# An mLSTM with a feed-forward layer: from chunk 8 on the state's part of the rows stays in PSUM

## The chip, the cores and the metric

The kernel runs on 1 core of one Trainium2 chip. The metric is the device time in microseconds (us), taken as the median over runs of the whole kernel. Engines are called by their short names: PE (TensorE, matmul), PEld (its weight loads), DVE (VectorE), ACT (ScalarE), POOL (GpSimd), SP (SyncE, which here only issues DMAs).

## What is computed

The reference, cut to its recurrence: 4 batches, 8 heads, 768 tokens, head width 40.

```python
for t in range(S):
    m_new = np.maximum(f_gate[:, :, t] + m, i_gate[:, :, t])
    f_stab = np.exp(f_gate[:, :, t] + m - m_new)
    i_stab = np.exp(i_gate[:, :, t] - m_new)
    m = m_new
    C = f_stab * C + i_stab * einsum('bhd,bhe->bhde', vt, kt)
    n = f_stab * n + i_stab * kt
    h_tilde = einsum('bhde,bhe->bhd', C, qt)
    nq = einsum('bhd,bhd->bh', n, qt)
    denom = np.maximum(np.abs(nq), 1.0)
    y[:, :, t] = sigmoid(o_gate[:, :, t]) * h_tilde / denom
...
h = x @ w_in                       # x: y as 3072 tokens x 320
g = np.maximum(h, 0.0) + alpha * np.minimum(h, 0.0)
return g @ w_out                   # 320 -> 2048 -> 320
```

## The kernel before

**Chunks and groups.** The recurrence is done in 24 chunks of 128 tokens (6 to a batch; `n` is the chunk, `c` its place in the batch). Within a chunk the rows come from decay-weighted scores, and what went before the chunk comes from a carried state. Two chunks make a group `g` of 256 tokens, and the feed-forward layer runs over 12 groups, in 8 steps of 256 features each: `up` (L563) makes 16 matmuls into one bank `ph`, then ACT, two DVE instructions at L585, ACT (`gh`, L593) and POOL (`gl`, L594) split the result, and `down` (L597) adds 12 matmuls per step into the two banks `po`.

**One chunk of attention from chunk 8 on** (`stage_b`, L402). For each half of the heads (`par`) ACT makes the decays `E` (L419), POOL masks them (L423), PE makes the scores `pS` (L435), DVE weighs them (L325), and ACT and DVE split them into three bf16 parts (L327, L328). Then `from_state` (L350) lets PE multiply the queries with the carried state into the PSUM bank `pI` (L364), and DVE scales that by the decay `eT` into the SBUF tile `T` (L367; a column of `eT` for each head is repeated over the 42 columns of the head). `values_by_parts` (L331) makes the rows of the chunk itself in two banks `pH` (L340), and DVE reduces these into the SBUF tile `S` (L344). L452 adds `S` to `T`. `gated_steps` (L378) takes the two columns of each head that carry plus and minus the denominator, takes the maximum of both and 1 (`r`, L386 in one instruction; where `c` is 0 there is no state, the rows are `S` alone, and L388 and L389 do it in two), takes the reciprocal (L390), multiplies it into the output gate `og` (L393, on POOL from chunk 6 on), and multiplies the rows with the gate into `xn` (L395, on DVE from chunk 8 on). POOL copies the last 64 columns of `xn` (L399). After a group's second chunk `stage_x` (L489) transposes `xn` on PE into two banks `p1`, `p2` (L463), and ACT and DVE split these (L482 to L486) for the feed-forward layer.

**Buffers.** All PSUM banks of the attention come from `psa` (L33): it takes two tags in turn, and each tag has two banks. So the fourth `psa` tile after a `pI` has the tag of `pI` again, and so has the second. A chunk takes them in this order: `pS` for par 0, [`p1`, `p2` of the group before], `pS` for par 1, `pI`, `pH` 0, `pH` 1, then `pu` of the next chunk's state update (L156). The SBUF tag `T` has two buffers, which `T`, `S` and `vr` (L313, the rest of the values of the next chunk, made on POOL at L315) share.

**Order of the work.** Attention runs as a side stream of the feed-forward layer (`Side`, L1113, and the loops from L1129): it goes two groups or so ahead. The order in which each engine issues its instructions is fixed when the program is built: a scheduler takes the instructions by priority, with durations that it estimates, and hands out a tag's buffers as they come free. On the chip every engine then follows its list in that order.

Of the kernel before, what the change touches and what calls it, by code (L numbers as in the profile page):

```python
# [8 lines left out]
F32 = mybir.dt.float32  # L9
# [4 lines left out]
ALU = mybir.AluOpType  # L14
# [3 lines left out]
def kernel(ctx: ExitStack, tc: tile.TileContext, q, k, v, i_gate, f_gate, o_gate, w_in, w_out, alpha, out):  # L18
    nc = tc.nc
    B, H, S, D = q.shape  # L20
    DM, DFF = w_in.shape
    P = 128
# [7 lines left out]
    VA = D + 2  # L30
# [4 lines left out]
    sb = ctx.enter_context(tc.tile_pool(name="sb", bufs=2))  # L35
# [6 lines left out]
    def psa(name):  # L42
        turns.reverse()
        return ps_a.tile([P, 512], F32, tag=turns[0], name=name)
# [34 lines left out]
    eT = const.tile([P, NC, BH], F32, tag="eT", name="eT")  # L79
# [131 lines left out]
    def state_parts(n):  # L211

        return C_t[2 - n % 2].rearrange("p h e -> p (h e)").bitcast(BF16).rearrange("p (s x) -> p s x", s=2)
# [81 lines left out]
    def values(n, E, busy=lambda: None):  # L295

        pH = psa(f"pH{n}")
        va = va_t[n // GC % NV][:, n % GC]
        for i in range(H):
            if i % 2 == 0:  # L300
                busy()
            par, p = divmod(i, NPR)
            h = 2 * p + par
            nc.tensor.matmul(
                pH[:, h * VA : (h + 1) * VA], E[par][:, p * P : (p + 1) * P], va[:, h], start=True, stop=True
            )
        return pH[:, : H * VA].rearrange("p (h e) -> p h e", e=VA)

    def value_parts(n):

        va = va_t[n // GC % NV][:, n % GC]
        V = late_pool.tile([P, H, 3, VA], BF16, tag="t", name=f"vb{n}", bufs=3)
        rest = sb.tile([P, H, VA], F32, tag="T", name=f"vr{n}")  # L313
        nc.scalar.copy(V[:, :, 0], va)
# [16 lines left out]
    def values_by_parts(n, Es):  # L331


        V = vbs.pop(n)
        S = sb.tile([P, H, VA], F32, tag="T", name=f"S{n}")
        for par in range(2):
            pH = psa(f"pH{n}_{par}")
            for p in range(NPR):
                for k, e in enumerate(Es[par]):
                    nc.tensor.matmul(  # L340
                        pH[:, p * 3 * VA : (p * 3 + 3 - k) * VA], e[:, p * P : (p + 1) * P],
                        V[:, 2 * p + par, : 3 - k], start=k == 0, stop=k == 2,
                    )
            nc.vector.tensor_reduce(  # L344
                by_parity(S, par), pH[:, : NPR * 3 * VA].rearrange("p (r k e) -> p r e k", k=3, e=VA),
                mybir.AxisListType.X, ALU.add,
            )
        return S

    def from_state(n, qf, Q=None):  # L350

        b, c = divmod(n, NC)
        pI = psa(f"pI{n}")
        if b == 0:
            C = C_t[(n - 1) % 3][:R].rearrange("p h e -> p (h e)")
            for p in range(NPR):
                es = slice(2 * p * VA, 2 * (p + 1) * VA)
                nc.tensor.matmul(pI[:, es], qf[:R, p * P : (p + 1) * P], C[:, es], start=True, stop=True)
        else:
            C = state_parts(n - 1)[: 3 * D]  # L360
            for h in range(H):
                es = slice(h * VA, (h + 1) * VA)
                for s in range(2):
                    nc.tensor.matmul(pI[:, es], Q[: 3 * D, s, h], C[:, s, es], start=s == 0, stop=s == 1)  # L364
        yield
        T = sb.tile([P, H, VA], F32, tag="T", name=f"T{n}")
        nc.vector.tensor_tensor(  # L367
            T, pI[:, : H * VA].rearrange("p (h e) -> p h e", e=VA),
            eT[:, c, b * H : (b + 1) * H].unsqueeze(2).broadcast_to([P, H, VA]), ALU.mult,
        )  # L370
        yield T

    def gated(n, hv):

        for _ in gated_steps(n, hv):
            pass

    def gated_steps(n, hv):  # L378
        b, c = divmod(n, NC)
        g, j = divmod(n, GC)  # L380
        if j == 0:
            xn_tiles[g] = sb.tile([P, GC, DM + KR], F32, tag="xn", name=f"xn{g}")
        xn = xn_tiles[g]
        r = sb.tile([P, H], F32, tag="r", name=f"r{n}")
        if c > 0:
            nc.vector.scalar_tensor_tensor(r, hv[:, :, D], 1.0, hv[:, :, D + 1], ALU.max, ALU.max)  # L386
        else:
            nc.vector.tensor_scalar(r, hv[:, :, D], 1.0, None, ALU.max)  # L388
            nc.vector.tensor_tensor(r, r, hv[:, :, D + 1], ALU.max)  # L389
        nc.vector.reciprocal(r, r)  # L390
        yield
        sg = o_tiles[b][:, c]
        (nc.gpsimd if n in SGP else nc.vector).tensor_tensor(sg, sg, r.unsqueeze(2).broadcast_to([P, H, D]), ALU.mult)  # L393
        yield
        (nc.gpsimd if c > 0 and n in XNP else nc.vector).tensor_tensor(  # L395
            xn[:, j, :DM].rearrange("p (h d) -> p h d", d=D), hv[:, :, :D], sg, ALU.mult
        )
        yield
        nc.gpsimd.tensor_copy(xn[:, j, DM:], xn[:, j, 2 * P : DM])  # L399
        yield  # L400

    def stage_b(n):  # L402
# [45 lines left out]
        if c > 0:  # L448
            *_, T = from_state(n, qf, Q)
        hv = values(n, Es) if n < NBF else values_by_parts(n, Es)  # L450
        if c > 0:
            nc.vector.tensor_tensor(T, T, hv, ALU.add)  # L452
            hv = T
# [82 lines left out]
    NBF = 8  # L536
# [253 lines left out]
    def first_group():  # L790
# [189 lines left out]
        def state_part():  # L980
            it = from_state(1, qk[1][0])
            next(it)
            yield
            got["T"] = next(it)
            yield
# [67 lines left out]
        add("u0m u0c", update_steps(0))  # L1053
        add("fsm fst", state_part())
        add("g0r g0g g0x g0p", lazily(lambda: gated_steps(0, got["h0"])))
        add("g1r g1g g1x g1p", lazily(lambda: gated_steps(1, got["T"])))
        add("s0a s0d", lazily(lambda: split_steps(0, slice(0, P), p1[0], p2[0])))
        add("s1a s1d", lazily(lambda: split_steps(0, slice(P, GT), p1[0], p2[0])))
# [132 lines left out]
```

## Time and profile before

| what | value |
|---|---|
| runs of the kernel before | 517.74, 509.68, 512.25 us; median 512.25 |
| the profiled execution | 514.26 us; span from its first to its last instruction 512.5 us |
| mean granted TensorE clock in it | 0.973 of full speed |
| busy share of PE, PEld, DVE, ACT, POOL | 96%, 91%, 65%, 62%, 59% |

Of a profiled execution every instruction has a start and a duration. "Idle before, releaser" tells how long the engine stood idle before an instruction and what ended that. Line numbers (L367) are those of the kernel before.

### The profile page before, as it was taken

The numbers are of one execution on the slowest core, as the hardware profiler recorded it, in microseconds if no ns is written. First come the engines' busy times: TensorE is split into PE (matmuls) and PEld (weight loads), VectorE is DVE, ScalarE is ACT, GpSimd is POOL, SyncE is SP. The second block draws the span as 40 slices with busy tenths as digits, with TensorE's granted clock in tenths as the row PEclk, the third lists the DMA queues.
The fourth block names the chain that finished last, engine by engine and source line by source line (L and its number), as shares of the span: only waits on it lengthen the run. The fifth ranks groups of instructions, "written<-read, shape, count | busy, mean of one in ns | idle before, by whom it ended". The sixth has DMA issues, their size and how long they took to land.

```text
span 512.5 us, 11748 instructions
## 1 busy us (share of the span) xinstructions
PE 490.2 (96%) x4455; PEld 469.0 (91%) x4455; DVE 334.3 (65%) x648; ACT 317.3 (62%) x687; POOL 304.2 (59%) x385
## 2 busy tenths in 40 slices
PE   8889989999999989999899999999998999999997
PEld 7778979999999989999789999999887999999997
DVE  7868999855444696785585687776676686652321
ACT  3839698655385667776976677686774664433332
POOL 6631154032197788859579789768866956333242
PEclk9878997999999999999999999999997999999999
DMA  9967977275068466487484664767642050000000
GB/s 170 239 135 223 245 190 209 68 144 127 1 145 203 95 162 140 81 185 161 108 170 100 149 143 104 162 159 130 152 136 61 30 115 2 1 27 1 27 1 26
DMA packets 171518, 60.58 MB, mean 118 GB/s; under 512 B 137990, under 2 KB 163958, under 8 KB 171462
## 3 DMA queue, kind: packets, MB, share of 16 engines
q1 hardware_dynamic: 171382, 59.73, 52.2%
q8 instruction: 35, 0.57, 0.5%
q14 instruction: 21, 0.17, 0.1%
q10 hardware_dynamic: 80, 0.11, 0.1%
HBM read 36.90 MB, written 4.03 MB: 80 GB/s over the span
## 4 chain that ended last, share of the span: by engine, by line
PE 67%; DVE 9%; POOL 8%; DMA 6%; ACT 4%; issue 4%; SPq 1%; ACTq 0%; POOLq 0%; DVEq 0%
PE po L602 25%; PE ph L572 4%; PE ph L578 3%; PE ph L575 3%; PE ph L573 3%; PE ph L576 3%; PE ph L577 3%; PE ph L574 3%; PE ph L579 3%; DMA kS<-Z 2%; POOL gl L594 2%; PE pH L340 2%; PE warm L929 2%; DMA wo<-in_moe_w_out_dram 2%; PE pS L435 2%
## 5 line engine op out<-in xcount | busy, mean ns | idle before, releaser
L594 POOL TENSOR_TENSOR gl<-g,gh 128x512 fp32r<-128x512 f32 x80 | 103.8, 1297 | 60.9 <-ACT gh L593 51.4
L585 DVE SCALAR_TENSOR_TENSOR g<-g,oma,ph 128x256 f32<-128x256 f32 x160 | 69.5, 475 | 76.7 <-ACT g L581 76.3
L602 PE MATMUL po<-OH,gh 128*128 128x320 f32 x352 | 107.8, 318 | 0.5 <-ACT gh L593 0.5
L602 PE MATMUL po<-OL,gh 128*128 128x320 f32 x352 | 105.2, 311 | 0.0
L581 ACT ACTIVATE g<-ph 128x512 f32<-128x512 f32 x96 | 57.1, 595 | 54.8 <-PE ph L579 43.2
L593 ACT CAST gh<-g 128x512 fp32r<-128x512 f32 x80 | 49.5, 619 | 38.6 <-DVE g L585 38.3
L602 PE MATMUL po<-OH,gl 128*128 128x320 f32 x352 | 68.8, 316 | 0.7 <-POOL gl L594 0.7
L602 PEld LDWEIGHTS po<-OH,gh 128*128 128x128 f32 x352 | 66.6, 190 | 1.0 <-ACT gh L593 0.9
L602 PEld LDWEIGHTS po<-OL,gh 128*128 128x128 f32 x352 | 66.4, 189 | 0.2 <-DVE OL L701 0.2
L572 PE MATMUL ph<-XH,WH 128*128 128x256 f32 x192 | 59.2, 308 | 3.0 <-DVE r L390 2.1
L423 POOL TENSOR_SCALAR_AFFINE_SELECT E<-E 128x512 f32<-128x512 f32 x44 | 31.3, 713 | 42.3 <-ACT E L419 39.2
L602 PEld LDWEIGHTS po<-OH,gl 128*128 128x128 f32 x352 | 55.0, 190 | 1.2 <-POOL gl L594 1.1
L576 PE MATMUL ph<-X,W 128*128 128x256 f32 x192 | 55.1, 288 | 0.0
L578 PE MATMUL ph<-XL,WH 128*128 128x256 f32 x192 | 54.8, 286 | 0.0
L573 PE MATMUL ph<-XH,WH 128*128 128x256 f32 x192 | 54.8, 285 | 0.0
L419 ACT ACTIVATE E<-Lb,bT 128x128 f32<-128x128 f32 x160 | 51.0, 393 | 6.0 <-PE pH L340 5.4
L575 PE MATMUL ph<-XH,WL 128*128 128x256 f32 x192 | 54.7, 285 | 0.0
L577 PE MATMUL ph<-XL,WH 128*128 128x256 f32 x192 | 54.6, 285 | 0.0
L574 PE MATMUL ph<-XH,WL 128*128 128x256 f32 x192 | 54.6, 284 | 0.0
L579 PE MATMUL ph<-X2L,W 128*128 128x256 f32 x192 | 54.6, 285 | 0.0
L327 ACT CAST E<-pS 128x512 bf16<-128x512 f32 x64 | 36.9, 581 | 19.2 <-DVE pS L328 10.8
L572 PEld LDWEIGHTS ph<-XH,WH 128*128 128x128 f32 x192 | 36.7, 191 | 4.0 <-issue 2.3
(194 smaller groups left out, 1200.0 us busy)
## 6 DMA issues: line engine op xcount, KB each, us to landing
Lb<-L_d SPq DMA_DIRECT2D x20, 512.0 KB
wo<-in_moe_w_out_dram SPq DMA_DIRECT2D x8, 640.0 KB
wi<-in_moe_w_in_dram SPq DMA_DIRECT2D x8, 512.0 KB
qn<-in_q_dram SPq DMA_DIRECT2D x24, 160.0 KB
kn<-in_k_dram SPq DMA_DIRECT2D x24, 160.0 KB
va<-in_v_dram SPq DMA_DIRECT2D x24, 160.0 KB
og<-in_o_gate_dram SPq DMA_DIRECT2D x24, 160.0 KB
out_dram<-ob SPq DMA_DIRECT2D x11, 320.0 KB
```

What stands on the lines that cost most here:

```text
L572: nc.tensor.matmul(dst, WH[half][:, 0, hs], XH[:, 0], start=True, stop=False)
L573: nc.tensor.matmul(dst, WH[half][:, 1, hs], XH[:, 1], start=False, stop=False)
L574: nc.tensor.matmul(dst, WL[half][:, 0, hs], XH[:, 0], start=False, stop=False)
L575: nc.tensor.matmul(dst, WL[half][:, 1, hs], XH[:, 1], start=False, stop=False)
L576: nc.tensor.matmul(dst, W2[:, fs], X2, start=False, stop=False)
L577: nc.tensor.matmul(dst, WH[half][:, 0, hs], XL[:, 0], start=False, stop=False)
L578: nc.tensor.matmul(dst, WH[half][:, 1, hs], XL[:, 1], start=False, stop=False)
L579: nc.tensor.matmul(dst, W2[:, fs], X2L, start=False, stop=True)
L581: nc.scalar.activation(gt, ph, AF.Relu, scale=-1.0)
L585: nc.vector.scalar_tensor_tensor(out=y[:, e], in0=gt[:, e], scalar=oma[:, f : f + 1], in1=ph[:, e], op0=ALU.mult, op1=ALU.add)
L594: (nc.vector if g < 2 else nc.gpsimd).tensor_tensor(gl, y, gh.bitcast(F32), ALU.subtract)
L602: nc.tensor.matmul(po[j], x[:, e, j * P : (j + 1) * P], W[f // NB][:, f % NB], **ends)
```

## The change

`T` is no tile of its own any more from chunk 8 (`NBF`) on: it is a view of the bank `pI`. L367 then writes back to where it reads, L452 adds `S` in that bank, and the maximum, and the product with the gate read the bank. Where `c` is over 0 the maximum takes two instructions (one tensor operand of each lies in PSUM) in place of one. Chunks 12 and 18 (`c` is 0) have no `T` and stay as they are, so 14 chunks are changed: 8 to 11, 13 to 17 and 19 to 23.

```diff
@@ from_state
         yield
-        T = sb.tile([P, H, VA], F32, tag="T", name=f"T{n}")
-        nc.vector.tensor_tensor(
-            T, pI[:, : H * VA].rearrange("p (h e) -> p h e", e=VA),
-            eT[:, c, b * H : (b + 1) * H].unsqueeze(2).broadcast_to([P, H, VA]), ALU.mult,
-        )
+        pI = pI[:, : H * VA].rearrange("p (h e) -> p h e", e=VA)
+
+        T = sb.tile([P, H, VA], F32, tag="T", name=f"T{n}") if n < NBF else pI
+        nc.vector.tensor_tensor(T, pI, eT[:, c, b * H : (b + 1) * H].unsqueeze(2).broadcast_to([P, H, VA]), ALU.mult)
         yield T
@@ gated_steps
         r = sb.tile([P, H], F32, tag="r", name=f"r{n}")
-        if c > 0:
+        if 0 < c and n < NBF:
             nc.vector.scalar_tensor_tensor(r, hv[:, :, D], 1.0, hv[:, :, D + 1], ALU.max, ALU.max)
         else:
             nc.vector.tensor_scalar(r, hv[:, :, D], 1.0, None, ALU.max)
```

## Rows read from the trace of the kernel before

**Rows 1.** Stretches: length, busy (count) of PE, PEld, DVE, ACT, POOL; PE clock; DMA.
```profile
150.00:450.00 300.00, 290.92 (x2894) 279.33 (x2893) 206.20 (x391) 200.24 (x450) 225.12 (x280) 0.99 0.54 119
...
386.80:393.00 6.20, 6.18 (x32) 5.92 (x33) 2.96 (x6) 2.30 (x5) 4.04 (x5) 0.50 0.22 44
```

**Rows 2.** Waits of PE between 150 and 450 us: total us, times, longest.
```profile
PE p L463 <- DVE xn L395: 2.7, 1, 2.7
PE pH L340 <- ACT E L327: 2.5, 2, 1.8
PE ph L572 <- DVE r L390: 2.1, 2, 1.6
PE ph L572 <- DVE g L585: 0.9, 3, 0.4
PE po L602 <- POOL gl L594: 0.7, 1, 0.7
```

**Rows 3.** DVE, POOL and PE in order of time, 183 to 187 us: start, duration.
```profile
183.11 2.21 DVE L386 SCALAR_TENSOR_TENSOR r<-T 128x8 f32<-128x8 f32 x1
185.24 0.86 DVE L585 SCALAR_TENSOR_TENSOR g<-g,oma,ph 128x256 f32<-128x256 f32 x2
...
184.51 0.78 POOL L236 TENSOR_TENSOR Z<-qr,Z 128x320 bf16<-128x320 f32 x1
186.29 0.72 POOL L393 TENSOR_TENSOR og<-og,r 128x320 f32<-128x320 f32 x1 [1.00 <-DVE r L390]
...
186.25 0.36 PE L572 MATMUL ph<-XH,WH 128*128 128x256 f32 x1 [1.59 <-DVE r L390]
```

**Rows 4.** The same engines, 382 to 388 us.
```profile
382.96 3.80 DVE L395 TENSOR_TENSOR xn<-T,og 128x320 f32<-128x320 f32 x1 [0.34 <-POOL og L393]
...
385.63 0.78 POOL L232 TENSOR_TENSOR kr<-kn,Z 128x320 f32<-128x320 f32 x1
386.38 1.02 POOL L318 TENSOR_TENSOR vb<-vr,vb 128x336 bf16<-128x336 f32 x1
...
386.82 0.69 PE L463 MATMUL p<-ident,xn 128*128 128x128 f32 x2 [2.70 <-DVE xn L395]
```

**Rows 5.** Single lines, whole span: duration ns min/median/max, first and last start.
```profile
L367 DVE TENSOR_TENSOR T<-pI,eT x20: 490/497/508, 27.8 to 445.3; 128x336 f32<-128x336 f32 x20
...
L395 DVE TENSOR_TENSOR xn<-T,og x15: 482/1050/3800, 35.0 to 450.7; 128x320 f32<-128x320 f32 x15
...
L395 DVE TENSOR_TENSOR xn<-pH,og x2: 483/487/491, 31.5 to 153.6; 128x320 f32<-128x320 f32 x2
...
L452 DVE TENSOR_TENSOR T<-T,S x14: 494/553/1649, 182.2 to 448.9; 128x336 f32<-128x336 f32 x14
L452 DVE TENSOR_TENSOR T<-T,pH x5: 490/503/505, 60.7 to 156.9; 128x336 f32<-128x336 f32 x5
...
L386 DVE SCALAR_TENSOR_TENSOR r<-T x20: 158/174/2208, 34.0 to 449.4; 128x8 f32<-128x8 f32 x20
...
L388 DVE TENSOR_SCALAR r<-pH x2: 156/160/165, 30.3 to 147.8; 128x8 f32<-128x8 f32 x2
...
L389 DVE TENSOR_TENSOR r<-r,pH x2: 161/162/163, 30.5 to 148.0; 128x8 f32<-128x8 f32 x2
```

**Rows 6.** DVE groups, 170 to 455 us: count, busy us, mean ns.
```profile
L325 DVE TENSOR_TENSOR pS<-pS,E 128x512 f32<-128x512 f32 x31 | 21.4, 694 | 3.8 <-PE pS L435 3.1
...
L395 DVE TENSOR_TENSOR xn<-T,og 128x320 f32<-128x320 f32 x14 | 19.1, 1365 | 2.1 <-POOL og L393 1.9
L452 DVE TENSOR_TENSOR T<-T,S 128x336 f32<-128x336 f32 x14 | 10.3, 737 | 0.3
L386 DVE SCALAR_TENSOR_TENSOR r<-T 128x8 f32<-128x8 f32 x14 | 8.0, 573 | 0.3
```

**Rows 7.** DVE and PE around the scores of chunk 20, 367 to 376 us.
```profile
367.75 0.50 DVE L367 TENSOR_TENSOR T<-pI,eT 128x336 f32<-128x336 f32 x1
...
374.93 0.67 DVE L344 TENSOR_REDUCE S<-pH 128x168 f32<-128x504 f32 x1
...
371.05 0.40 PE L435 MATMUL pS<-qS,kS 120*128 120x128 bf16 x4
```

## The prediction, made before the changed kernel ran

> **What bounds the kernel now.** I read the busy time by stretch first. Between 150 and 450 us, where the changed chunks run, PE is busy for 290.92 of 300 us [rows 1], so PE sets the pace, and all that an edit of DVE's work can give back is what PE lost there: 9.1 us of standing still, and what it lost at a lower clock. [...] Together 12.2 us, 2.4% of the time, is the ceiling. After 450 us hardly any attention is left.
>
> Next the waits of PE in that stretch say who released it [rows 2]: `xn` 2.7, `E` (ACT) 2.5, `r` 2.1, `g` 0.9, `gl` 0.7 us, together 8.9 of the 9.1. Two of the five are lines that the change touches, or stand behind such lines.
>
> Then the order of time at these two shows what they are. At 183.11 us the maximum over 8 columns (`r`, L386) takes 2.21 us where the shortest of its kind takes 0.158 [rows 3, 5]. It reads two columns of `T`, both in SBUF. It ends at 185.32, within 0.04 us of the end of POOL's instruction `Z` (184.51 + 0.78 = 185.29), after which POOL stands still [rows 3]. `g` for the next `ph` is queued behind it on DVE, and PE waits 1.59 us. At 382.96 the product `xn` (L395, `T` and `og` in SBUF) takes 3.80 us instead of 0.48 and ends at 386.76, just after POOL changed from `kr` to `vb` at 386.4, and that `vb` then takes 1.02 us; PE waits 2.70 us for `xn` [rows 4, 5]. Over the whole span the three lines with both inputs in SBUF spread widely (L395 482 to 3800 ns, L452 494 to 1649, L386 158 to 2208), while their twins with one input in PSUM do not: L395 from `pH` 483 to 491, L452 with `pH` 490 to 505, L367 490 to 508 over 20 instances [rows 5]. I read this as: a DVE instruction with two inputs in SBUF waits for POOL's running instructions, one with a PSUM input does not.
>
> [...]
>
> **The change, part by part.** 14 chunks are changed.
>
> `xn` (L395): one input now in PSUM. 14 took 19.1 us [rows 6]; 14 x 0.487 [rows 5] is 6.8. DVE gains 12.3.
>
> The sum (L452): one input now in PSUM. 14 took 10.3 [rows 6]; 14 x 0.503 is 7.0. Gain 3.3. It writes to PSUM now, as L367 does. L325 works in place in PSUM in 694 ns for 512 columns [rows 6]; for 336 that gives 455 ns in proportion, and 694 at most. I keep 0.50 for both lines; the worst end would cost 2 x 14 x 0.19 = 5.4 us of DVE.
>
> The maximum: 14 instances took 8.0 [rows 6]; now L388 at 0.160 and L389 at 0.162 with an input in PSUM [rows 5], 14 x 0.322 = 4.5. Gain 3.5, though there are 14 more instructions.
>
> So DVE is busy about 19.1 us less. DVE is not the bound (206 of 300 us [rows 1]), so this is worth only what PE waited for:
>
> - The wait at 184.7 us: `r` gives back 2.21 - 0.32 = 1.89 us, more than the 1.59 that PE stood. Gone. A second such wait makes up the 2.1 of the group [rows 2]: 2.1 - 1.6 = 0.5 us. Gone. Together 2.1.
> - The wait of 2.70 us: `xn` would end at 382.96 + 0.49 = 383.45, and PE came to the transposes at 386.82 - 2.70 = 384.12. Gone, with 0.7 us in hand. If that cover fails (the gate on POOL comes later), as much of it returns as the gate is late.
> - The low clock behind it: 3.1 us. It followed this wait, and nothing else there stands as long. Gone.
> - What is late next: `E` on ACT (2.5), `g` (0.9) and `gl` (0.7) [rows 2]. I leave these as they are; bounds 0 to 4.1 us of further gain.
>
> Sum: 2.1 + 2.7 + 3.1 = 7.9 us.
>
> **What is added** is a longer hold on a bank. `pI` was free once L367 had read it; now it is held until `xn`, through POOL's gate. At chunk 19 that is from 368.25 [rows 7] to 386.76, and still to 383.45 with the faster `xn`. The fourth tile after it, the scores of the next chunk, has the same tag, and must take the tag's other bank, which the second `pH` holds until its reduction (L344). At chunk 20 PE began the scores at 371.05, and that reduction ended at 375.60 [rows 7]: 4.55 us too early for the new order. By the same reading the scores of the next chunk come before that reduction after 5 of the 14 chunks (8, 15, 17, 19, 21), by 0.7 to 4.6 us, 11.7 in all. At the other nine the bank is free in time. PE has feed-forward matmuls that need no such bank, and the build draws a new order in which they go first; behind the waiting scores stand, on PE, the next `up` and `down`, and ACT and POOL wait for these. Bounds: 0 where other matmuls are put ahead, 11.7 where PE stands still at each. I take 0, nearest to the 9.1 us that all of PE's waits came to with the same kind of planned order, and keep the other end for a rival. A group's second `p` bank also waits for `xn` now, but its transposes are 0.4 us of PE work, and no use before `xn` is there.
>
> In SBUF the tag `T` loses its one long holder, so `vr` on POOL no longer can wait for `xn`; POOL stood idle elsewhere, so I count nothing (0 to 1 us).
>
> The new order behind chunk 8 can also shift waits by chance. I allow 3 us either way, a third of what PE's order costs now.
>
> The profiled execution took 514.26 us, 512.5 of it span. 514.26 - 7.9 = 506.4. It lies 2.0 us above the median of 512.25, from which the same step gives 504.4. I forecast the middle, 505.4 us, 1.3% to 1.5% faster. What a measurement of this kernel can tell from no change is about 2%, so this most likely counts as no difference.
>
> **The rivals.**
>
> A, more than these two waits: `g`, `E` and `gl` sit on chains that pass through DVE too, and 19 us less of DVE work, and POOL instructions that are no longer held up (`vb` 1.02), shorten them all. For: DVE's `g` waits are behind these stretched lines. Against: the longest `E` wait is released by ACT. Price: the whole ceiling, 12.2 us: 514.26 - 12.2 = 502.1, or 500.1 from the median; call it 501.
>
> B, the room is not where PE needs it: after the stretched lines go, PE waits at the same places for the gate on POOL or for ACT, and only the shorter half of the gain is left: 2.1 us. Then 512.2, or 510.2 from the median; call it 511.
>
> C, slower: the bank. PE stands at the scores until the reduction at all five places, 11.7 us, and at the two longest (4.6 and 2.8, both as long as the 2.70 that cost a clock fall) the clock falls, 2 x 3.1 = 6.2. 17.9 - 7.9 is 10.0 us slower: 524.3, or 522.3 from the median. It decides from the point where PE stands for more than 7.9 us, about two thirds of the 11.7, without any fall of the clock. For: the order is planned with estimated durations, and DVE's reduction is late behind `g` and copies. Against: PE has other matmuls ready at almost all times.
>
> D, it does not do what it says: the stretch does not come from the second SBUF input. Then nothing is gained, and 14 more small instructions cost 2.3 us of DVE that PE hardly sees: 514. Against: 20 instances of L367 that never pass 508 ns [rows 5].
>
> **How the numbers follow.** Forecast 0.53, A 0.18, B 0.13, C 0.12, D 0.04. The forecast's own range is 500 to 510 (3 us by order, and the 2 us between the scales). Toward A the range goes to 498, toward C to 518, where about half of C's chance is left out. Faster by over 2% (below 502): most of A and a little of the forecast, 0.24. Slower by over 2% (above 522.5): half of C and a little by chance, 0.08. Within: 0.68.
>
> **What would show it.** Right: L395, L452 and the two lines of the maximum stay below 0.52 and 0.17 us in all changed chunks, DVE's busy time falls by some 19 us, PE has no wait for `xn` or `r` above 0.5 us, and the clock stays at 1.00 from 150 us on. The step on the bank is wrong if PE waits at L435 for L344, or at L364 for `xn`. [...] The whole is wrong if PE's idle time from 150 to 450 us stays near 9 us.

## The result and the profile after

The changed kernel takes 503.06 us (median of 6 runs, 501.28 to 506.35), the kernel before 510.99 us (median of 6, 509.54 to 517.74). The ratio is 0.9869, with a 95% interval of 0.9832 to 0.9905: 1.3% faster, clear of no change, though less than 2%. A ratio counts only executions within 1.5% of the fastest of their kernel; a median in microseconds counts all. The profiled execution took 503.71 us, 502.0 of it span, against 514.26 and 512.5.

The busy time of PE over 150 to 450 us, in the columns of [rows 1], then PE's waits in that stretch (total, times, longest), which answer to [rows 2]:

```profile
150.00:450.00 300.00, 296.33 (x2969) 285.55 (x2968) 192.16 (x415) 203.60 (x454) 224.38 (x283) 1.00 0.55 119
```
```profile
PE pH L340 <- ACT E L327: 2.3, 1, 2.3
PE ph L571 <- DVE g L584: 1.0, 2, 0.9
```

PE stands still for 3.7 us where it was 9.1. The waits for `xn` and behind `r` are gone, and with them the low clock: the granted clock of the stretch is 1.00. What is left is one wait of 2.3 us for ACT and 1.0 us for `g`. What the low clock had cost can be read at PE's `up` matmuls in the kernel before, at a granted clock of 0.50 (the first two lines) and of 1.00 (the last two):

```profile
391.77 0.41 PE L577 MATMUL ph<-XL,WH 128*128 128x256 f32 x1
391.98 0.41 PE L578 MATMUL ph<-XL,WH 128*128 128x256 f32 x1
...
397.16 0.28 PE L577 MATMUL ph<-XL,WH 128*128 128x256 f32 x1
397.28 0.28 PE L578 MATMUL ph<-XL,WH 128*128 128x256 f32 x1
```

From 389.21 to 392.20 us such matmuls start 213 ns apart, from 396.57 to 397.40 us 118 ns. By that ratio the 6.2 us at 0.50 lost an estimated 2.8 us. Standing still and clock together give 5.4 + 2.8 = 8.2 us.

The changed lines (numbers are one or two off those of before: L369 was L367, L451 was L452, L387 and L388 are the maximum, L394 was L395), first over the whole span (duration min/median/max), which answers to [rows 5], then as groups from 170 to 455 us, which answers to [rows 6]:

```profile
L369 DVE TENSOR_TENSOR pI<-pI,eT x14: 505/516/517, 174.6 to 434.7; 128x336 f32<-128x336 f32 x14
...
L451 DVE TENSOR_TENSOR pI<-pI,S x14: 515/517/517, 180.4 to 438.3; 128x336 f32<-128x336 f32 x14
...
L387 DVE TENSOR_SCALAR r<-pI x14: 158/166/168, 180.9 to 438.9; 128x8 f32<-128x8 f32 x14
...
L388 DVE TENSOR_TENSOR r<-r,pI x14: 153/161/163, 181.9 to 439.1; 128x8 f32<-128x8 f32 x14
...
L394 DVE TENSOR_TENSOR xn<-pI,og x14: 478/484/492, 185.3 to 441.2; 128x320 f32<-128x320 f32 x14
...
L394 DVE TENSOR_TENSOR xn<-S,og x2: 537/880/1224, 254.2 to 356.2; 128x320 f32<-128x320 f32 x2
```
```profile
L451 DVE TENSOR_TENSOR pI<-pI,S 128x336 f32<-128x336 f32 x14 | 7.2, 516 | 0.5
...
L394 DVE TENSOR_TENSOR xn<-pI,og 128x320 f32<-128x320 f32 x14 | 6.8, 485 | 2.8 <-POOL og L392 2.6
...
L387 DVE TENSOR_SCALAR r<-pI 128x8 f32<-128x8 f32 x14 | 2.3, 165 | 0.4
...
L388 DVE TENSOR_TENSOR r<-r,pI 128x8 f32<-128x8 f32 x14 | 2.2, 160 | 0.4
```

No instance of a changed line is stretched: the product is 478 to 492 ns where it was 482 to 3800. The last row of the first view is the control inside the kernel: in the two chunks without a state part the same product still has both inputs in SBUF, and one of its two instances takes 1224 ns. DVE's time for the three lines is 7.2 + 6.8 + 2.3 + 2.2 = 18.5 us, where it was 10.3 + 19.1 + 8.0 = 37.4 [rows 6].

What a stretched line waits for can be read off where it ends. In the kernel before, from chunk 8 on, all 8 maxima of 0.48 us or more end 0.02 to 0.03 us after the end of a POOL instruction that ran meanwhile, and all 7 sums of 0.60 us or more and all 11 products of 0.61 us or more end 0.34 to 0.40 us after one. One of these maxima in the kernel before, with POOL's instructions:

```profile
417.32 1.47 DVE L386 SCALAR_TENSOR_TENSOR r<-T 128x8 f32<-128x8 f32 x1
...
417.94 0.82 POOL L315 TENSOR_TENSOR vr<-va,vb 128x336 f32<-128x336 f32 x1
418.73 0.81 POOL L206 TENSOR_TENSOR C<-cw,C 40x336 bf16<-40x336 f32 x1
```

It ends at 418.79 us, 0.03 us after `vr`. The product of 3.80 us saw four POOL instructions in a row end before its own turn came. Over all runs below and the two kernels, 207 instances of these lines with no input in PSUM took more than 0.2 us (8 columns) or 0.56 us (320 and 336 columns), and every one ends 0.01 to 0.04 or 0.34 to 0.41 us after a POOL instruction. In the change, 56 of the 70 instances of the five lines above that read `pI` overlap a POOL instruction, and none of them is stretched. So in these runs it is POOL that the lines wait for, and an input in PSUM takes them out of that wait.

The bank, which is held longer, read in order of time (DVE, then PE) at chunks 8 and 9:

```profile
179.10 0.68 DVE L344 TENSOR_REDUCE S<-pH 128x168 f32<-128x504 f32 x1 [1.21 <-PE pH L340]
...
181.91 1.07 PE L434 MATMUL pS<-qS,kS 120*128 120x128 bf16 x16
```

The scores of chunk 9 now come after the reduction that frees the tag's other bank, as they had to. At all five places the new order does that, and nowhere does PE wait for it.

### The profile page after: what moved, and what is told of

Read it like the earlier page. It is cut to its first block, busy times and chain, and to the rows that moved or that the text cites. A ratio compares the mean times of both kernels' runs of the same rounds, so it can differ in the third digit from the quotient of the medians.

```text
span 502.0 us, 11746 instructions
## 1 busy us (share of the span) xinstructions
PE 484.0 (96%) x4455; PEld 463.7 (92%) x4455; DVE 315.5 (63%) x662; ACT 317.6 (63%) x687; POOL 299.8 (60%) x385
## 4 chain that ended last, share of the span: by engine, by line
PE 79%; ACT 6%; DVE 6%; DMA 3%; issue 2%; POOL 2%; SPq 1%; ACTq 0%; DVEq 0%; POOLq 0%
PE po L601 31%; PE ph L571 5%; PE ph L574 4%; PE ph L577 4%; PE ph L572 4%; PE ph L575 4%; PE ph L576 4%; PE ph L578 4%; PE ph L573 4%; PE pS L434 3%; PE pH L340 3%; PE pH L304 2%; ACT E L418 2%; PE pu L161 2%; PE p L462 1%
```

## The experiments

"Order" means the order in which each engine issues its instructions. Every ratio is to the kernel before on the same chip, with its 95% interval. "Port theory" is the author's name for the reading that a DVE instruction with two inputs in SBUF waits for POOL; that they share a port is shown by no run.

**1. One half each, and each kind of hold alone.** Only the sum from PSUM (e1_sum_only; chunks from 8 on, the edits are to the changed kernel):

```diff
-            nc.vector.tensor_tensor(T, T, hv, ALU.add)
-            hv = T
+            rows = sb.tile([P, H, VA], F32, tag="T", name=f"W{n}") if n >= NBF else T
+            nc.vector.tensor_tensor(rows, T, hv, ALU.add)
+            hv = rows
...
-        if 0 < c and n < NBF:
+        if c > 0:
```

> Only the sum reads PSUM: the scaled state part stays in its bank, the sum with S goes into an SBUF tile of tag T, and the maximum (one instruction) and the product with the gate read that tile, both with two inputs in SBUF. Port theory (a DVE instruction with two SBUF inputs waits for POOL, and PE waits behind it): the sum stays at or below 0.52 us in all 14 chunks, the maximum and the product spread again up to 1.5 us and more, and as PE's waits hung on those two, most of the gain is gone: 508 to 511 us where before is 511 and the change 503. Rival (the gain is the new order of the instructions or the freed buffers, not the durations): the order is new here too, so 503 to 506 us, whatever the durations.

Measured: 504.47 us, ratio 0.9882 [0.9838, 0.9927]. The durations came as the port theory has it, the time as the rival has it:

```profile
L394 DVE TENSOR_TENSOR xn<-W,og 128x320 f32<-128x320 f32 x14 | 19.5, 1394 | 1.6 <-POOL og L392 1.6
...
L385 DVE SCALAR_TENSOR_TENSOR r<-W 128x8 f32<-128x8 f32 x14 | 8.0, 570 | 0.4
...
L452 DVE TENSOR_TENSOR W<-pI,S 128x336 f32<-128x336 f32 x14 | 7.1, 508 | 0.7
```

The product and the maximum are as long as before, yet PE waits for neither in that profile (its waits are 2.8 us for `g`, 1.8 for `E`, 1.0 for `gh` and 0.2 for `gl`). A long instruction costs where PE hangs behind it, and in this order no row of PE names one. The order is new as well, so it had to be held fixed, which groups 2 and 4 do.

The maximum and the product from PSUM alone (e2_rows_only):

```diff
-        T = sb.tile([P, H, VA], F32, tag="T", name=f"T{n}") if n < NBF else pI
+        T = sb.tile([P, H, VA], F32, tag="T", name=f"T{n}")
...
+        banks[n] = pI
...
-            nc.vector.tensor_tensor(T, T, hv, ALU.add)
-            hv = T
+            rows = banks[n] if n >= NBF else T
+            nc.vector.tensor_tensor(rows, T, hv, ALU.add)
+            hv = rows
```

> The other half alone: the scaled state part goes to an SBUF tile again, the sum has two SBUF inputs and writes into the bank, and the maximum and the product with the gate read the bank. Port theory: the sum spreads again between 0.5 and 1.6 us (some 10 us in all against 7.2 in the change), the maximum and the product stay short, and nearly all of the gain stays: 503 to 505 us. Rival (the sum's share is what counts, or the short life of T in SBUF): 507 us and more.

Measured: 504.81 us, 0.9864 [0.9808, 0.992]; the sum took 12.8 us (915 ns each, where some 10 us in all were expected), the product 6.8. The time is as the port theory expects.

The kernel before, with the bank held (e3_hold_only; `xn` is read so that it comes last):

```diff
+        banks[n] = pI
...
+        if c > 0 and n >= NBF:
+            nc.vector.tensor_tensor(r[:, :1], banks[n][:, :1], xn[:, j, :1], ALU.max)
```

> The kernel before, with the bank of the state part held until the product with the gate, by one more DVE instruction of one column that reads it there. It has the cost of the change without its gain. Port theory with the bank at no cost, as predicted: 510 to 513 us, the stretched lines as before, and PE never waits at the scores for the reduction. Rival C (the bank costs): 515 us and more, with PE waits at the scores. Rival order (the longer hold draws another order, and that was the gain): 503 to 506 us.

Measured: 509.41 us, 0.9966 [0.9929, 1.0003]. The hold costs nothing that can be seen, and its new order brings nothing clear either. PE never waits at the scores; what it waits for in this order is above all `g`:

```profile
PE ph L577 <- DVE g L590: 5.9, 4, 3.6
PE pH L340 <- ACT E L327: 2.9, 2, 2.1
PE pH L340 <- DVE r L402: 0.3, 1, 0.3
```

The longest of these waits, while chunk 18 is under way, hangs on a stretched product by a longer way, here DVE, SP, ACT and PE in order of time:

```profile
339.78 1.91 DVE L398 TENSOR_TENSOR xn<-T,og 128x320 f32<-128x320 f32 x1
...
341.73 4.15 SPq L122 DMA_DIRECT2D og<-in_o_gate_dram  x6
...
350.65 1.28 ACT L126 ACT_TABLE_LOAD   x1 [2.92 <-DMA og<-in_o_gate_dram]
...
356.25 0.57 ACT L586 ACTIVATE g<-ph 128x512 f32<-128x512 f32 x1
...
357.88 0.55 PE L577 MATMUL ph<-XH,WH 128*128 128x256 f32 x1 [3.61 <-DVE g L590]
```

The product of chunk 17 is the last reader of its batch's output gate, and the gate tile has one buffer. So the load of the next batch's gate is issued only when that product has ended, at 341.69 us; ACT stands 2.92 us for it, and the instruction that `g` needs is queued behind it on ACT. Behind PE's wait the granted clock is 0.50 (357.9 to 363.9 us).

The change, with a buffer of the SBUF tag `T` held as long as before (e4_sbuf_hold):

```diff
+        if n >= NBF:
+            holds[n] = sb.tile([P, H, VA], F32, tag="T", name=f"W{n}")
+            nc.vector.tensor_copy(holds[n][:, 0, :1], pI[:, 0, :1])
...
+        if n in holds:
+            nc.vector.tensor_scalar(hv[:, 0, :1], hv[:, 0, :1], holds[n][:, 0, :1], None, ALU.mult)
```

> The change, with a buffer of the SBUF tag T held from the scaling to the product with the gate, as the tile T held it before, by two more DVE instructions of one column whose tensor input lies in PSUM. Port theory: the freed buffer was worth nothing, 502 to 505 us, the changed lines all short. Rival (the freed buffer lets POOL and ACT go ahead and made the gain): 507 us and more, with waits of POOL at the values' rest (vr).

Measured: 501.91 us, 0.9837 [0.979, 0.9885]. The freed SBUF buffer was worth nothing. (The second new instruction overwrites one column of the bank after its last use; no output depends on it.)

**2. Operands and order crossed.** An order is given here only to kernels that hold no more buffers than the one that it was drawn for. The last two runs hold the bank and, in one case, the buffer too, so their orders suit both sets of operands: order A is that of e4_sbuf_hold, order B that of e3_hold_only. The edit chains every engine's instructions in a written list:

```diff
+    for engine, steps in orders.items():
+        ...
+            tc.add_manual_dep(
+                i, last.name,
+                mybir.DependencyInfo(mybir.DependencyClass.NoSync, mybir.DependencyReason.DATA), reason="order",
+            )
```

> The operands of the kernel before (T in SBUF, sum, maximum and product with two SBUF inputs), but every engine issues its instructions in the order of e4_sbuf_hold (501.9 us, where these lines are short). Only the operands differ from that run. Port theory: the three lines spread again, PE waits behind them, 508 to 512 us. Rival (the order made the gain): 501 to 504 us, in spite of the long lines.

> The operands of the change (everything in the bank), but in the order of e3_hold_only (509.4 us, where these lines are long and the bank is held as here). Only the operands differ from that run. Port theory: the lines are short, the waits for g of 5.9 us in that order go, 502 to 505 us. Rival (order): 508 to 511 us, in spite of the short lines.

| | all three lines long (SBUF) | all short (PSUM) |
|---|---|---|
| order A | 0.9953 [0.9914, 0.9992], 510.24 us | 0.9837 [0.979, 0.9885], 501.91 us |
| order B | 0.9966 [0.9929, 1.0003], 509.41 us | 0.9892 [0.984, 0.9944], 506.02 us |

Along a row only operands differ (and a few instructions of one column): 1.2% and 0.7%. In order A the two intervals lie apart. In order B they overlap by 0.0015, and the short run lies above the 502 to 505 us expected, so this row supports the first and would not be enough alone. Down a column only the order differs: 0.1% and 0.6%, with intervals that overlap. So the operands make the gain; an order's share, if there is one, is not shown. In order A, long, the groups of DVE (170 to 455 us) and then PE's waits are

```profile
L396 DVE TENSOR_TENSOR xn<-T,og 128x320 f32<-128x320 f32 x14 | 20.6, 1473 | 3.7 <-POOL og L394 3.5
...
L387 DVE SCALAR_TENSOR_TENSOR r<-T 128x8 f32<-128x8 f32 x14 | 12.0, 858 | 0.4
...
L453 DVE TENSOR_TENSOR T<-T,S 128x336 f32<-128x336 f32 x14 | 11.4, 811 | 0.2
```
```profile
PE p L464 <- DVE xn L396: 3.1, 2, 1.9
PE pH L341 <- ACT E L328: 2.4, 2, 2.0
PE ph L573 <- DVE g L586: 1.6, 3, 0.8
PE pH L341 <- DVE E L329: 0.8, 2, 0.5
```

and in the same order, short, the waits are

```profile
PE pH L340 <- ACT E L327: 2.3, 1, 2.3
PE ph L578 <- DVE g L591: 1.1, 2, 0.8
```

The wait for the product is the row that comes and goes with the operands. In order B, short, the chain at chunk 18 is gone: the sums of chunk 17 still start at the same time in both runs (333.38 and 333.31 us), but the product is short, the gate's load is issued 2.2 us earlier, and ACT no longer waits for it. Of the waits for `g`, which were expected to go, 3.5 us are left:

```profile
338.81 0.48 DVE L395 TENSOR_TENSOR xn<-pI,og 128x320 f32<-128x320 f32 x1
...
339.53 4.14 SPq L123 DMA_DIRECT2D og<-in_o_gate_dram  x6
```
```profile
PE ph L572 <- DVE g L585: 3.5, 4, 2.0
PE pH L341 <- ACT E L328: 2.5, 3, 1.4
```

**3. A spare sum, long or short**, in one and the same order (the spare result is not read):

```diff
+                spare = sb.tile([P, H, VA], F32, tag="T", name=f"W{n}")
+                nc.vector.tensor_tensor(spare, hv, hv, ALU.add)
```

In the control the sum is `(spare, T, hv)`, with `T` in PSUM.

> The change with one spare sum more in each of its 14 chunks, just before the sum: S plus S into an SBUF tile that nothing reads, both inputs in SBUF. Port theory: the spare sum takes 0.5 to 1.6 us (10 us in all, as the sum did before), 3 us more than in e6_spare_psum, and the time lies 1 to 4 us above that run. Rival (the stretch only matters by the order, or DVE has room for all of it): equal to e6_spare_psum within 1 us.

> The control: the same spare sum in the same place, and all engines in the same order as e5_spare_two_sbuf, but one input lies in PSUM (the scaled state part plus S). Port theory: 0.51 us each, 7.2 us of DVE in all, which has the room: 502 to 505 us, as the change. Rival (DVE's busy time itself counts): 506 us and more.

Measured: 505.2 us, 0.9883 [0.9833, 0.9934], and the control 506.06 us, 0.9903 [0.9872, 0.9934]. The durations differ as expected, first the run, then the control:

```profile
L453 DVE TENSOR_TENSOR W<-S 128x336 f32<-128x336 f32 x14 | 10.0, 713 | 0.4
```
```profile
L453 DVE TENSOR_TENSOR W<-pI,S 128x336 f32<-128x336 f32 x14 | 7.1, 508 | 0.6
```

The time does not: the port theory's 1 to 4 us did not come, though the intervals leave room for some 2 us. The 2.9 us of stretch in front of the sum found room on DVE, as far as can be told. The control, at 506.06 us, lies where its rival (DVE's busy time itself counts) had it and not at the 502 to 505 expected; its interval overlaps that of the change, so that rival is not excluded for 7.1 us more of DVE work. What the rows show is that the stretch follows the operands; that it costs time everywhere is not shown.

**4. Which line carries the gain, in order A.** The edits are those of group 1, and for the last one the maximum alone from SBUF:

```diff
+        elif c > 0:
+            two = sb.tile([P, H, 2], F32, tag="two", name=f"two{n}")
+            nc.vector.tensor_copy(two, hv[:, :, D:])
+            nc.vector.scalar_tensor_tensor(r, two[:, :, 0], 1.0, two[:, :, 1], ALU.max, ALU.max)
```

> Only the sum reads PSUM, as in e1_sum_only, but in the order of e4_sbuf_hold, in which all short gave a ratio of 0.9837 and all long 0.9953. Theory as predicted (PE's waits hang on the product and the maximum, which are long here): 0.992 to 0.996, 507 to 510 us. Rival that e1_sum_only suggests (every stretched line counts, and the sum, on DVE ahead of both, carries a good part): 0.986 to 0.990, 504 to 507 us.

> Only the maximum and the product read PSUM, as in e2_rows_only, in the order of e4_sbuf_hold; the sum has two SBUF inputs and is long. Theory as predicted: 0.983 to 0.987, 502 to 505 us. Rival (the sum carries a good part): 0.988 to 0.992, 505 to 508 us.

> The sum and the product read PSUM; of the rows, the two columns of the denominator are copied to SBUF first, and the maximum reads both from there in one instruction. Order of e4_sbuf_hold. Theory as predicted: the maximum is long again (up to 2 us, 8 to 12 us in all) and costs PE 2.1 us: 503 to 505 us, ratio 0.987 to 0.989. Rival (the maximum alone costs nothing): 0.983 to 0.985.

| in order A | ratio | interval | us |
|---|---|---|---|
| all long | 0.9953 | 0.9914 to 0.9992 | 510.24 |
| sum short, maximum and product long | 0.9928 | 0.9893 to 0.9963 | 506.76 |
| sum and product short, maximum long | 0.9884 | 0.9826 to 0.9942 | 505.98 |
| maximum and product short, sum long | 0.9844 | 0.979 to 0.9897 | 503.52 |
| all short | 0.9837 | 0.979 to 0.9885 | 501.91 |

With the order fixed, the sum alone gives at most little, and the maximum and the product alone give all that can be told. The profile says the same: with the sum short, PE still has its wait for the product, 2.3 us:

```profile
PE p L464 <- DVE xn L395: 2.3, 2, 1.4
```

What the maximum gives by itself stays open: its run lies between, with an interval over both neighbours, and the maximum came out at 5.0 us in all, not the 8 to 12 that was expected, so it is a weaker dose than in the kernel before. No wait of PE for it stands in that profile.

**5. A version meant to be faster.** In the changed kernel PE's one long wait left is at chunk 12. ACT and then PE, in order of time:

```profile
239.95 1.28 ACT L126 ACT_TABLE_LOAD   x1 [1.89 <-DMA og<-in_o_gate_dram]
241.25 1.80 ACT L126 ACTIVATE og<-og 128x1920 f32<-128x1920 f32 x1
...
244.70 0.23 PE L340 MATMUL pH<-vb,E 128*128 128x126 bf16 x1 [2.31 <-ACT E L327]
```

ACT stands for the gate's load, and the casts of `E` are queued behind the sigmoid.

```diff
+        if n % NC == 0:
+            S = psa(f"S{n}")[:, : H * VA].rearrange("p (h e) -> p h e", e=VA)
...
-            if c == 0 and par == 1:
-                open_gate(b)
...
+        if c == 0:
+            open_gate(b)
         gated(n, hv)
```

> The change, plus two more edits: the rows of chunks 12 and 18, which have no state part, are reduced into a PSUM bank too, and the output gate of a new batch goes through the sigmoid after the chunk's scores are weighed in place of before. If the wait of 2.3 us that PE has left at chunk 12 comes from ACT standing behind the gate's load, it goes: 500 to 502 us. Rival (the wait moves to the product of chunk 12, as the gate is late there): 503 to 505 us.

Measured: 504.62 us, 0.9839 [0.9785, 0.9893], not to be told from the change. The wait for ACT is gone, and others are there instead:

```profile
PE pS L435 <- DVE S L347: 1.7, 1, 1.7
PE ph L574 <- DVE g L587: 1.4, 2, 0.8
PE pH L343 <- DVE XL L487: 1.1, 1, 1.1
PE po L604 <- POOL gl L596: 0.3, 1, 0.3
```

So neither the 500 to 502 us forecast nor the rival's wait for the product came. The first row is the predicted price of the bank: 1.7 us at the scores, behind a reduction of `S` (DVE itself had stood 3.05 us for ACT just before). In the change no place paid it; with one more tile held, one does.

## Why the prediction was right

- The time: forecast 505.4, measured 503.06, and the difference of the medians is 7.9 us, as the sum had it (7.9). That it fits to the tenth is luck: the interval of the ratio stands for 4.9 to 8.6 us. By the profiled pair the difference is 10.6; 1.4 of that arises before the changed chunks, since DVE's first copy of a finished group starts at 122.3 us in place of 123.7.
- The waits: 2.1 and 2.7 us were to go, and are gone [rows 2]. The clock at 386.8 us was to go with them, and did. But that price is one execution's: in order A, long, the waits for `xn` are followed by no low clock at all (1.00 from 150 to 450 us), and of the two spare runs, both with a wait of 2.8 us for `E` at 247 us, one then has 0.50 (246.6 to 250.0 us) and the other 1.00. What the clock gives back on average stays open. No run shows the 3.1 us that the sum has for the clock (nor the ceiling of 12.2 us and the 6.2 us of rival C, which are made with it): it takes half of the 6.2 us at 0.50 [rows 1] as lost, and the starts of the `up` matmuls, 213 ns apart there and 118 ns at 1.00, show some 2.8 us in its place. `E` was to stay at some 2.5 and is 2.3, `g` at 0.9 and is 1.0; only `gl`, 0.7, went besides.
- The durations: 18.5 us for the three lines against the 18.3 worked out, and DVE's busy time by the two pages fell by 18.8 (334.3 to 315.5), against 19.1.
- The step from two inputs in SBUF to a wait for POOL: right. All 207 stretched instances end behind a POOL instruction, and of the change's 70 with an input in PSUM, 56 of them beside a POOL instruction, none is stretched. What DVE and POOL share there, no run shows.
- The bank at no cost: no row of PE names it in the change, and the hold alone, with an order of its own, leaves the kernel before where it was (0.9966). Rival C's place exists, as the last experiment shows, but it needed a tile more.
- The chances: A (the whole ceiling) did not come, since `E` and `g` stayed; B did not, since nothing took the place of the waits; D fell with the durations.
- One step is too simple. The sum took the two waits of one profile as the price of the stretched lines. Other orders of the same operands have other waits: 5.9 us for `g` in order B, of which the longest came through the gate's load, and 3.1 for `xn` in order A; with only the sum short, in a new order, PE waited for neither line. What the comparisons say is that such lines cost some 4 to 7 us (0.7% in order B, 1.2% in order A, 1.3% between the two kernels, of 511); that it would be these two waits was that order's own.
- The price of the maximum, 2.1 us in the sum, stays unproven by itself.

## What to carry to other kernels

A line whose shortest and longest instances differ several times over (here 482 to 3800 ns), while its twin with another kind of operand does not (478 to 492 ns), points at what the operands share, not at the work. See whether such instances end with an instruction of another engine (here 0.01 to 0.04 or 0.34 to 0.41 us after one of POOL): that names what they wait for. Shorten the line where the engine that sets the pace hangs behind it, be it by way of a buffer that the line frees late; elsewhere no cost of the stretch was seen here (505.2 us with 10.0 us of spare sums, 506.06 us with 7.1). Before a gain is put down to an edit in a kernel whose order is drawn anew at each build, hold the order fixed and change the operands alone.

## What was not expected

- One SBUF input can be enough. The maximum of chunks 12 and 18 reads `S` by a TENSOR_SCALAR of 8 columns with one tensor input; it took 305 and 636 ns in the change and 2200 ns on average in the run with only the rows short, while the same form from PSUM never passed 168. With `S` in PSUM (the last experiment) it is 166. RECIPROCAL, with one SBUF input too, never passed 204 in either kernel. The TENSOR_SCALAR, too, waits for POOL: every instance of this form over 0.2 us, in any of the runs, ends 0.02 to 0.03 us after the end of a POOL instruction, the two in the change and the longest (3.95 us, in the run with only the rows short) among them. Why this form is stretched with one SBUF input and RECIPROCAL is not, no run here tests.
- Writing PSUM instead of SBUF cost little, if anything: in the change the scaling takes 516 against 497 ns, the sum 517 against 503 for its form with one PSUM input (medians), but in the two spare runs the same sum takes 510 and 505 ns on average. The prediction's bounds reached to 694.
- The granted clock ahead of chunk 8 differs for the same work. Two runs of order A that do the same work until then had these stretches (columns of [rows 1]), with 0.93 in the run with the sum short, which comes first, and 0.66 in the run with the maximum and the product short:

```profile
20.00:35.00 15.00, 13.06 (x106) 11.58 (x102) 13.23 (x31) 9.51 (x18) 6.82 (x8) 0.93 1.04 197
```
```profile
20.00:35.00 15.00, 14.26 (x97) 13.20 (x97) 10.56 (x22) 6.69 (x13) 5.51 (x6) 0.66 1.06 211
```

  Their first stores of an output group were issued at 121.1 and 125.8 us. So single profiles of this kernel are compared from chunk 8 on, and times only over several runs.
